# A softmax maximum by transposes, first rows tile by tile, and a new order in a transformer block's forward and backward pass

## The chip, the cores and the metric

The kernel runs on one core of a Trainium2 chip. The metric is the device time of one execution in microseconds (us). A core has five engines with a queue each: TensorE (PE in the profile, its weight loads PEld), VectorE (DVE), ScalarE (ACT), GpSimd (POOL) and SyncE (SP), which only issues transfers. Every engine takes its instructions strictly in the order of its queue and waits on semaphores for the others.

## The reference

One transformer block over 2048 positions of width 512, its output, and the gradients of the input and of all weights for a given output gradient. In bf16:

```
ln1  = layernorm(x);  q, k, v = ln1 @ wqkv            # 32 heads of 16
logit[s, w] = q[s] . k[s - 2w] / 4,  w = 0..7          # a dilated window, masked where s - 2w < 0
attn = softmax over w;  o[s] = sum over w of attn[s, w] * v[s - 2w]
h    = x + o @ wo
out  = h + gelu(layernorm(h) @ w1 + b1) @ w2 + b2      # width 1792 inside
outputs: out, and d(x), d(wqkv), d(wo), d(w1), d(b1), d(w2), d(b2) for grad_out
```

The softmax runs over only eight values for each head and position.

## The kernel before

The positions are cut into four chunks of 512, each of four row tiles of 128. Every chunk passes through: layernorm and turning (`p1_ln`), projections (`p1_qkv`), windowed attention (`p1_attn`), its output (`p1_o`), `wo` and the second layernorm (`p1_h`), the feed-forward part forward (`p2_h`, `p2_out`), its derivative (`p2_dg`) and backward (`p2_bwd`), the backward attention (`p3_go`, `p3_dots`, `p3_bands`, `p3_gl1`); at the end come the weight gradients (`wg_ffn`), whose matmuls also fill TensorE beside the backward attention.

**Order and homes.** The Python code only describes operations: each call of `op` names an engine, a function that issues the instructions, and the buffers read and written. A planner's result is written into the file as two tuples: `TURN` is the order in which all operations are issued (so each engine's queue is the part of it that belongs to that engine), `HOMES` the address of every SBUF buffer and the PSUM bank (0 to 7) of every PSUM buffer, in the order in which buffers are made. With these tuples present nothing is planned at run time.

**First rows.** For chunk 0, `layernorm` takes statistics of each tile on VectorE (L577, L578), adds epsilon (ve, L583), raises to the power -1/2 on GpSimd (L585) for two tiles at a time, forms minus mean times deviation (nm, L586) on VectorE, and normalizes each tile with a scale and a bias (L596). `to_fm_pairs` turns the tiles two by two on TensorE (L628, 8 transposes into one bank) and ScalarE copies 1024 columns of a pair out. `spin` runs idle matmuls on zeros (L1283): `WARM` = (11, 4) says 11 at the very start and 4 behind the turning. A transpose and a copy bring the bias b1 into columns (L1306, L1307).

**Attention.** `dots` multiplies q by eight shifted views of k on VectorE (L672) and TensorE sums within heads (L679) into two PSUM banks `L`: partitions are 4 shifts by 32 heads, the two banks hold the other factor two of the eight shifts. The maximum over the shifts: ScalarE copies one bank (asb), VectorE takes the maximum of both (m1, L856, 128 partitions); ScalarE copies the upper 64 partitions down (m1h, L860), VectorE takes the maximum (m2, L861); ScalarE copies 32 partitions down (m2h, L865), VectorE again (m3, L866). TensorE subtracts it from both banks with a matrix of -1 (L870, two matmuls of 512 columns), ScalarE takes the exponential (L872), TensorE sums (L878), VectorE inverts and so on.

**Bands.** The products with shifted rows, forward (`o`) and backward (`q`, `v`, `k`), go through `band`, 64 times in all: rows come by a gather on GpSimd's queue, VectorE multiplies 4096 values for each partition (L698, 2.3 us), TensorE sums eight matmuls of 512 columns into a bank (L707), ScalarE copies the bank out (L712). Two bands (m = 0, 1) make one half of a chunk, which TensorE then turns back (L722, `unperm`).

**Other lines that are spoken of:** L804 and L821 projections, L956 and L958 first feed-forward matmul and the copy of its bank by ScalarE, L961 GELU, L1012 second feed-forward matmul, L926 addition of b2 to h, L650 and L615 other transposes, L1201 weight gradients.

Of the kernel before, what the change touches and what calls it, by code (L numbers as in the profile page):

```python
# [427 lines left out]
def kernel(  # L428
# [142 lines left out]
    def layernorm(c, src, MV, ST, VE, NM, R, mv, st, ve, nm, rs, dst, eng, n=TPC):  # L571
# [8 lines left out]
        for j0 in range(0, TPC, n):  # L580
# [4 lines left out]
            op("POOL", 1.1, lambda s=s: G.tensor_tensor(out=rs[:, s], in0=ve[:, s], in1=mhalf[:, 0:n], op=ALU.pow), r=[(VE, (c, j0))], w=[(R, (c, j0))], tag="pow")  # L585
            op("DVE", 0.16, lambda s=s: V.scalar_tensor_tensor(out=nm[:, s], in0=mv[:, s, 0], scalar=-1.0, in1=rs[:, s], op0=ALU.mult, op1=ALU.mult),  # L586
               r=[(R, (c, j0))] + [(MV, t) for t in ts], w=[(NM, (c, j0))], tag="nm")
        for j in range(TPC):
            t = c * TPC + j
            rk = [(src, j), (R, (c, j // n * n)), (NM, (c, j // n * n))]  # L590
# [4 lines left out]
            else:  # L595
                op("DVE", 0.36, lambda t=t, j=j: V.tensor_scalar(out=dst()[:, j, :], in0=src()[:, j, :], scalar1=rs[:, t:t + 1],  # L596
                                                                scalar2=nm[:, t:t + 1], op0=ALU.mult, op1=ALU.add),
# [22 lines left out]
    def to_fm_pairs(src, dst, tag):  # L620

        for jp in range(2):
            pt = ps_("pt" + tag, 1, "pt", 2)

            def tr(jp=jp, pt=pt):
                for dc in range(DC):
                    for j in range(2):
                        T.transpose(pt.bf()[:, dc * 256 + j * P:dc * 256 + (j + 1) * P], src()[:, 2 * jp + j, dc * P:(dc + 1) * P], ident[:])  # L628
            op("PE", 8 * XP, tr, r=[(src, 2 * jp), (src, 2 * jp + 1)], w=[pt], tag="xp" + tag, al=[dst])
            evict(dst, lambda jp=jp: dst()[:, :, jp * 256:(jp + 1) * 256], pt, lambda pt=pt: pt.bf().rearrange("p (a n) -> p a n", a=DC), 1024,  # L630
                  key=jp, tag="fm" + tag)
# [60 lines left out]
    def band(cf, R, sc, m, sgn, dst, at, sca, tag):  # L692
        pr = sb("prb" + tag, [P, 2, 4, 512], tag="prod", lim=4)
        o0 = (2 if sgn < 0 else 0) + 4 * m
        st = -1024 if sgn < 0 else 1024

        def prod():
            V.tensor_tensor(out=pr().rearrange("p a j (d h) -> p a j d h", h=H),  # L698
                            in0=_sub(R()[:, o0, 0:1], [[st, 2], [512, 4], [32, DH], [1, H]]),
                            in1=_sub(cf()[:, 2 * sc + m, 0, 0, 0:1], [[128, 2], [32, 4], [0, DH], [1, H]]), op=ALU.mult)  # L700
        op("DVE", tt_us(4096), prod, r=[R, cf], w=[pr], tag="prod" + tag)
        ps = ps_("bs" + tag, 1, "bs", 2)

        def sums():
            for hf in range(2):
                for j in range(4):
                    T.matmul(ps()[32 * j:32 * j + 32, :], lhsT=S32[:], rhs=pr()[:, hf, j, :], start=(hf == 0), stop=(hf == 1),  # L707
                             skip_group_check=True)
        op("PE", 0.45, sums, r=[CST, pr], w=[ps], tag="bsum" + tag, al=[dst])

        def out():
            A.activation(out=dst()[:, at, :].rearrange("p (h d) -> p h d", d=DH), in_=ps().rearrange("p (d h) -> p h d", h=H),  # L712
                         func=ACT.Copy, scale=sca)
        op("ACT", act_us(512), out, r=[ps], w=[(dst, at)], tag="sink" + tag)
# [860 lines left out]
```

## Time and profile before

| what | value |
|---|---|
| three runs | 584.12 us median (582.18 to 587.52) |
| the profiled execution | 582.24 us, span 580.5 us |
| granted TensorE clock, mean | 0.997 |
| TensorE busy | 556.8 us, 96% of the span |
| VectorE busy | 490.2 us, 84% |
| ScalarE busy | 351.6 us, 61% |
| GpSimd busy | 90.4 us, 16% |
| DMA | 150.99 MB, mean 260 GB/s |

The span runs from the first to the last instruction. In a timeline row stand the start, the length, engine, line, operation, output and inputs, the shape (partitions x elements), how many instructions are merged, and in brackets the idle time of the engine before it with what ended it. In a row of groups stand busy time, mean length in ns, and idle time before. A matmul of 512 columns shows 0.38 us from start to modelled end, but the next one starts 0.216 us after it.

### The profile page before, as it was taken

To read this page: it belongs to the slowest core of one execution; us is meant where nothing else is said; L and a number is where in the kernel's file an instruction comes from. 1 tells how busy PE (TensorE), PEld (TensorE's weight loads), DVE (VectorE), ACT (ScalarE), POOL (GpSimd) and SP (SyncE) were. 2 spreads that over 40 slices of the span, in tenths; PEclk is the share of its full clock that TensorE was granted. 3 is DMA by queue.
4 is the path that set the end of the run, shared out by engine and by line. 5 is a ranking of instruction groups with operands and counts; after the bars stand their busy time and mean duration, and the time that the engine had idled before them with its cause. 6 is when DMAs were issued, how large, how long until landed. Compare 5 with 4: busy or idle time off the path is not lost.

```text
span 580.5 us, 9212 instructions
## 1 busy us (share of the span) xinstructions
PE 556.8 (96%) x3525; PEld 261.3 (45%) x3579; DVE 490.2 (84%) x645; ACT 351.6 (61%) x517; POOL 90.4 (16%) x89
## 2 busy tenths in 40 slices
PE   7999989799899999999999999999999899999997
PEld 3454544244344444444545444444444446444443
DVE  7999799999999999789865999998998899973900
ACT  5588899998997885988453424136542455364111
POOL 3020605031000000000000100432421241400000
PEclk8999999999999999999999999999999999999999
DMA  8579699999999998989999989989989996879322
GB/s 256 148 254 322 230 260 355 250 189 299 227 260 269 244 279 131 258 239 273 282 233 273 324 298 283 311 316 292 345 342 314 322 311 244 313 235 362 114 73 72
DMA packets 163147, 150.99 MB, mean 260 GB/s; under 512 B 112768, under 2 KB 149536, under 8 KB 158240
## 3 DMA queue, kind: packets, MB, share of 16 engines
q1 hardware_dynamic: 156768, 103.22, 64.1%
q0 software_dynamic: 6336, 47.19, 23.1%
q8 instruction: 28, 0.46, 0.3%
q14 instruction: 15, 0.12, 0.1%
HBM read 78.25 MB, written 42.77 MB: 208 GB/s over the span
## 4 chain that ended last, share of the span: by engine, by line
PE 75%; issue 4%; DVE 4%; ACT 3%; DMA 2%; SPq 0%; ACTq 0%; DVEq 0%
PE ps L1201 25%; PE ps L1060 8%; PE ps L1012 8%; PE ps L1173 7%; PE ps L1037 7%; PE ps L956 6%; PE ps L707 4%; PE ps L1082 2%; PE ps L722 2%; DMA gk_d<-gks 1%; PE ps L679 1%; DVE prbo L698 1%; PE ps L918 1%; ACT xb L958 1%; PE ps L650 1%
## 5 line engine op out<-in xcount | busy, mean ns | idle before, releaser
L956 PE MATMUL ps<-ln2T,w 128*128 128x512 bf16 x224 | 53.5, 379 | 2.5 <-ACT xb L958 2.3
L1037 PE MATMUL ps<-goT,w2T 128*128 128x512 bf16 x215 | 54.1, 379 | 0.4
L1012 PE MATMUL ps<-w,gl 128*128 128x512 bf16 x217 | 51.9, 379 | 0.9 <-ACT xb L958 0.6
L1201 PE MATMUL ps<-gw1in,ln2b 128*128 128x512 bf16 (+1 forms) x256 | 52.6, 353 | 0.0
L1060 PE MATMUL ps<-w1T,xb 128*128 128x512 bf16 x220 | 50.6, 379 | 0.2
L1201 PE MATMUL ps<-gor,gw2in 128*128 128x512 bf16 x217 | 50.2, 379 | 0.4 <-issue 0.2
L1039 DVE SCALAR_TENSOR_TENSOR xb<-xb,ps 128x512 bf16<-128x512 bf16 x56 | 37.9, 683 | 14.6 <-PE ps L1037 13.6
L1173 PE MATMUL ps<-wqkvT,gqkvT 128*128 128x512 bf16 x184 | 42.7, 379 | 0.6 <-issue 0.3
L958 ACT ACTIVATE xb<-ps,b1c 128x512 bf16<-128x512 f32 x56 | 36.7, 686 | 7.3 <-PE ps L956 7.2
L698 DVE TENSOR_TENSOR prbk<-Rk,cfk 128x4096 bf16<-128x4096 bf16 x16 | 36.0, 2288 | 6.0 <-DMA Rk<-q_d,rowi 2.7
L564 ACT CAST wgs<-ps 128x512 bf16<-128x512 f32 (+1 forms) x30 | 16.6, 559 | 38.8 <-PE ps L1201 38.7
L698 DVE TENSOR_TENSOR prbv<-Rv,cfv 128x4096 bf16<-128x4096 bf16 x16 | 36.3, 2287 | 3.3 <-PE ps L1201 1.8
L698 DVE TENSOR_TENSOR prbq<-Rq,cfq 128x4096 bf16<-128x4096 bf16 x16 | 36.3, 2278 | 2.3 <-PE ps L707 0.8
L672 DVE TENSOR_TENSOR prf<-qt,kt 128x4096 bf16<-128x4096 bf16 x16 | 35.9, 2278 | 1.4 <-PE ps L707 0.7
L672 DVE TENSOR_TENSOR prb<-got,vw 128x4096 bf16<-128x4096 bf16 x16 | 36.1, 2280 | 1.2 <-DMA vw<-v_d 0.6
L698 DVE TENSOR_TENSOR prbo<-Ro,cfo 128x4096 bf16<-128x4096 bf16 x16 | 36.2, 2286 | 0.3
L661 POOL DMA_INDIRECT Rq<-k_d,rowi x8 | 15.5, 1940 | 130.2 <-PE ps L1012 103.4
L737 ACT ACTIVATE gyr<-ps,rstd 128x512 bf16<-128x512 f32 x32 | 21.9, 685 | 21.5 <-PE ps L1173 18.5
L1201 PEld LDWEIGHTS <-ln2b 128*128 128x128 bf16 x256 | 24.0, 98 | 23.8 <-issue 3.4
L956 PEld LDWEIGHTS <-w 128*128 128x128 bf16 x224 | 21.1, 98 | 29.9 <-issue 5.6
L980 ACT ACTIVATE xb<-xb 128x2048 bf16<-128x2048 bf16 (+1 forms) x16 | 27.1, 1695 | 11.9 <-DVE xb L979 11.9
L1201 PEld LDWEIGHTS <-gw2in 128*128 128x128 bf16 x224 | 21.2, 98 | 27.4 <-issue 3.4
(178 smaller groups left out, 1069.8 us busy)
## 6 DMA issues: line engine op xcount, KB each, us to landing
g_d<-xrg SPq DMA_DIRECT2D x12, 512.0 KB
gh_d<-xrh SPq DMA_DIRECT2D x12, 512.0 KB
gw2in<-g_d SPq DMA_DIRECT2D x3, 2048.0 KB
gw1in<-gh_d SPq DMA_DIRECT2D x3, 2048.0 KB
ln_d<-ln SPq DMA_DIRECT2D x8, 512.0 KB
w<-in_B_w_dram SPq DMA_DIRECT2D x2, 1792.0 KB
out_dram<-wgs SPq DMA_DIRECT2D x13, 256.0 KB
v_d<-tmv SPq DMA_DIRECT2D x8, 256.0 KB
```

Source lines behind the costliest of these rows:

```text
L672: op("DVE", tt_us(4096), lambda g=g, pr=pr: V.tensor_tensor(out=pr(), in0=ql()[:, g, :].unsqueeze(1).to_broadcast([P, W, 512]), in1=_sub(k ...
L698: V.tensor_tensor(out=pr().rearrange("p a j (d h) -> p a j d h", h=H), in0=_sub(R()[:, o0, 0:1], [[st, 2], [512, 4], [32, DH], [1, H]]), i ...
L707: T.matmul(ps()[32 * j:32 * j + 32, :], lhsT=S32[:], rhs=pr()[:, hf, j, :], start=(hf == 0), stop=(hf == 1), skip_group_check=True)
L956: T.matmul(ps(), lhsT=w1()[:, dc, f * P:(f + 1) * P], rhs=cols(ln2T[c], dc, c in FM2), start=(dc == 0), stop=(dc == DC - 1))
L958: op("ACT", act_us(512, 1), lambda f=f, ps=ps, xb=xb, f0=f0: A.activation(out=xb()[:, f - f0, :], in_=ps(), func=ACT.Identity, bias=b1c[:, ...
L980: op("ACT", act_us(N), lambda xb=xb: A.activation(out=fl(xb), in_=fl(xb), func=ACT.Tanh, scale=GC), w=[xb], tag="tanh", mode=2)
L1012: T.matmul(ps(), lhsT=d["g"][f // 4]()[:, f % 4, j * P:(j + 1) * P], rhs=w2()[:, f, :], start=(f == 0), stop=(f == FT - 1))
L1037: T.matmul(ps(), lhsT=w2T()[:, dc, f * P:(f + 1) * P], rhs=goT()[:, dc, :], start=(dc == 0), stop=(dc == DC - 1))
L1039: op("DVE", 0.70, lambda f=f, ps=ps, z=z, f0=f0: V.scalar_tensor_tensor(out=z()[:, f - f0, :], in0=z()[:, f - f0, :], scalar=1.0, in1=ps() ...
L1060: T.matmul(ps(), lhsT=d["d"][f // 4]()[:, f % 4, j * P:(j + 1) * P], rhs=w1T()[:, f, :], start=(f == 0), stop=(f == FT - 1))
L1173: T.matmul(ps(), lhsT=d["gqkv"]()[:, b, j * P:(j + 1) * P], rhs=wqkvT()[:, b, :], start=(i == 0 and b == ks[0]), stop=(i == 2 and b == ks[ ...
L1201: T.matmul(ps()[:, 0:N], lhsT=l, rhs=r, start=(n == 0), stop=(n == k - 1))
```

## The change

- Softmax maximum: m1h, m2, m2h and the old m3 are gone. TensorE turns m1 in four transposes into a PSUM bank (xpm); one VectorE reduction with a negated maximum over the four shifts reads that bank and gives m3, now 128 positions by 4 tiles by 32 heads. The subtraction becomes 32 matmuls of 128 columns with the new m3 as weights, each into 32 output partitions.
- First rows: chunk 0 forms its deviations for three tiles and then for one; a tile is turned alone (`to_fm_tiles`) and copied alone, the fourth copy on VectorE. Where VectorE normalizes, it subtracts the mean and multiplies by the deviation as two scalars, and nm is no longer formed.
- Bands: `bands` makes both products and both sums of a half and then one ScalarE operation: a single instruction over both banks where these are neighbours, else two.
- The bias transpose (b1t, b1c) moves behind the first rows; `WARM` becomes (17, 4).
- `TURN` and `HOMES` are replaced as a whole (1988 operations instead of 2029).

```diff
-    def layernorm(c, src, MV, ST, VE, NM, R, mv, st, ve, nm, rs, dst, eng, n=TPC):
+    def layernorm(c, src, MV, ST, VE, NM, R, mv, st, ve, nm, rs, dst, eng, split=0):
...
-        for j0 in range(0, TPC, n):
+        first = [split if split and j >= split else 0 for j in range(TPC)]
+        for j0 in sorted(set(first)):
+            n = first.count(j0)
...
+            if "ACT" in eng:
+                op("DVE", 0.16, lambda s=s: V.scalar_tensor_tensor(out=nm[:, s], in0=mv[:, s, 0], scalar=-1.0, in1=rs[:, s], op0=ALU.mult, op1=ALU.mult),
...
-                op("DVE", 0.36, lambda t=t, j=j: V.tensor_scalar(out=dst()[:, j, :], in0=src()[:, j, :], scalar1=rs[:, t:t + 1],
-                                                                scalar2=nm[:, t:t + 1], op0=ALU.mult, op1=ALU.add),
+                op("DVE", 0.36, lambda t=t, j=j: V.tensor_scalar(out=dst()[:, j, :], in0=src()[:, j, :], scalar1=mv[:, t, 0:1],
+                                                                scalar2=rs[:, t:t + 1], op0=ALU.subtract, op1=ALU.mult),
...
+    def to_fm_tiles(src, dst, tag):
+        for j in range(TPC):
             pt = ps_("pt" + tag, 1, "pt", 2)
+            def tr(j=j, pt=pt):
                 for dc in range(DC):
+                    T.transpose(pt.bf()[:, dc * P:(dc + 1) * P], src()[:, j, dc * P:(dc + 1) * P], ident[:])
+            op("PE", DC * 0.057, tr, r=[(src, j)], w=[pt], tag="xp" + tag, al=[dst])
+            evict(dst, lambda j=j: dst()[:, :, j * P:(j + 1) * P], pt, lambda pt=pt: pt.bf()[:, 0:512].rearrange("p (a n) -> p a n", a=DC), 512,
+                  key=j, eng="DVE" if j == 3 else "ACT", tag="fm" + tag)
...
+    def bands(cf, R, sc, sgn, dst, at, sca, tag):
+        two = []
+        for m in range(2):
...
+        def out():
+            p0, p1 = two
+            if abs(p1.home - p0.home) == 1:
+                A.activation(out=dst()[:, at:at + 2, :].rearrange("p m (h d) -> p m h d", d=DH),
+                             in_=_sub(p0(), [[(p1.home - p0.home) * BANK, 2], [1, H], [H, DH]]), func=ACT.Copy, scale=sca)
+                return
+            for m in range(2):
+                A.activation(out=dst()[:, at + m, :].rearrange("p (h d) -> p h d", d=DH), in_=two[m]().rearrange("p (d h) -> p h d", h=H),
+                             func=ACT.Copy, scale=sca)
+        op("ACT", 2 * act_us(512), out, r=two, w=[(dst, at), (dst, at + 1)], tag="sink" + tag)
...
-        m1, m1h, m2, m2h, m3 = sb("m1", [P, 512]), sb("m1h", [64, 512]), sb("m2", [64, 512]), sb("m2h", [32, 512]), sb("m3", [32, 512])
+        m1, m3 = sb("m1", [P, 512]), sb("m3", [P, 4, 32])
...
+        def turn():
+            for j in range(4):
+                T.transpose(mt.bf()[:, j * P:(j + 1) * P], m1()[:, j * P:(j + 1) * P], ident[:])
+        op("PE", 0.23, turn, r=[CST, m1], w=[mt], tag="xpm")
+        op("DVE", tt_us(512, True), lambda: V.tensor_reduce(out=m3(), in_=_sub(mt.bf()[:, 0:1], [[P, 4], [1, 32], [32, 4]]), axis=mybir.AxisListType.X,
+                                                            op=ALU.max, negate=True), r=[mt], w=[m3], tag="m3")
         def sub():
             for hf in range(2):
-                T.matmul(L()[:, hf * 512:(hf + 1) * 512], lhsT=nSum4[0:32, :], rhs=m3(), start=False, stop=True, skip_group_check=True)
+                for j in range(4):
+                    for w4 in range(4):
+                        T.matmul(L()[32 * w4:32 * w4 + 32, hf * 512 + j * P:hf * 512 + (j + 1) * P], lhsT=m3()[:, j, :], rhs=ident[:],
+                                 start=False, stop=True, skip_group_check=True)
...
-WARM = (11, 4)
+WARM = (17, 4)
```

More of the change, by code (lines that the diff above doesn't have):

```diff
@@ L1304 @@
     load(B2C, lambda: b2bc[:], lambda: _ap(B_b2, [[0, P], [1, D]]), 128, tag="b2")
-    pb = ps_("pb1")
-    op("PE", 0.1, lambda: T.transpose(pb.bf()[:, 0:FT], b1b[:], ident[0:FT, 0:FT]), r=[B1B], w=[pb], tag="b1t")
-    op("DVE", 0.2, lambda: V.tensor_copy(out=b1c[:], in_=pb.bf()[:, 0:FT]), r=[pb], w=[B1C], tag="b1c")
     for c in range(NC):
```

77 lines of the change are left out of this document (29 added, 48 removed), and 249 rows, old and new, of tables (HOMES, TURN).

## The prediction

> **What bounds the kernel now.** I read the page first (span, busy shares, chain), then the busy time in stretches of 20 us, then the timeline of the stretches in which TensorE (PE) falls short, and last the groups of instructions by line and shape for the durations.
>
> ```profile
> span 580.5 us, 9212 instructions
> ...
> PE 556.8 (96%) x3525; PEld 261.3 (45%) x3579; DVE 490.2 (84%) x645; ACT 351.6 (61%) x517; POOL 90.4 (16%) x89
> ...
> PE 75%; issue 4%; DVE 4%; ACT 3%; DMA 2%; SPq 0%; ACTq 0%; DVEq 0%
> ```
>
> TensorE is busy for 556.8 of 580.5 us, and the chain that ended last runs over it for 75%. So 23.7 us are all that can be won without taking work from TensorE, and the question is where they lie.
>
> ```profile
> 0.00:20.00 20.00, 15.72 (x69) 7.31 (x71) 15.88 (x43) 10.79 (x22) 4.99 (x23) 0.91 0.73 212
> ...
> 100.00:120.00 20.00, 16.16 (x112) 6.81 (x112) 19.42 (x24) 19.13 (x23) 2.27 (x2) 1.00 1.11 259
> ...
> 140.00:160.00 20.00, 16.99 (x84) 7.32 (x85) 19.79 (x36) 19.88 (x22) 0.00 (x0) 1.00 0.95 234
> ...
> 460.00:480.00 20.00, 18.23 (x143) 8.90 (x143) 19.13 (x15) 8.83 (x16) 7.38 (x6) 1.00 0.89 317
> ...
> 560.00:580.00 20.00, 16.73 (x76) 7.45 (x76) 0.00 (x0) 4.50 (x8) 0.00 (x0) 1.00 0.19 66
> ```
>
> The columns after the length are busy time of PE, its weight loads, DVE (VectorE), ACT (ScalarE) and POOL (GpSimd), then granted clock and DMA. Five stretches hold 16.2 us of the 23.7: 4.3 at the start, 3.8 at 100 to 120, 3.0 at 140 to 160, 1.8 at 460 to 480, 3.3 at the end. At 100 to 120 DVE is full, at 140 to 160 DVE and ACT both are. The waits themselves:
>
> ```profile
> 106.84 0.61 PE L707 MATMUL ps<-prbo,S 128*32 128x512 bf16 x8 [1.59 <-DVE prbo L698]
> ...
> 109.04 0.62 PE L707 MATMUL ps<-prbo,S 128*32 128x512 bf16 x8 [0.61 <-DVE prbo L698]
> 111.24 0.61 PE L707 MATMUL ps<-prbo,S 128*32 128x512 bf16 x8 [1.59 <-DVE prbo L698]
> ...
> 156.70 1.02 PE L956 MATMUL ps<-ln2T,w 128*128 128x512 bf16 x4 [2.35 <-ACT xb L958]
> ...
> 159.80 1.46 PE L1012 MATMUL ps<-w,gl 128*128 128x512 bf16 x6 [0.56 <-ACT xb L958]
> ...
> 462.71 1.05 PE L707 MATMUL ps<-prbk,S 128*32 128x512 bf16 x16 [1.66 <-DVE prbk L698]
> ```
>
> Until 111 us TensorE waits for VectorE's band products of the third chunk (L698): up to there VectorE's queue sets the pace, and only what shortens that queue counts. At 156 us TensorE waits for ScalarE to empty a bank (L958): there ScalarE's queue counts. From 160 on a microsecond of TensorE work is a microsecond of span.
>
> **The start.**
>
> ```profile
> 1.87 3.97 PE L1283 MATMUL ps<-wz 128*128 128x512 bf16 x11 [1.87 <-DVE wz L1284]
> ...
> 6.41 0.17 DVE L583 TENSOR_SCALAR ve<-mv 128x2 f32<-128x2 f32 x1
> ...
> 7.38 0.18 PE L1306 MATMUL ps<-ident,b1b 14*128 14x14 bf16 x1 [1.54 <-POOL rstd L585]
> 7.59 0.17 DVE L1307 CAST b1c<-ps 128x14 f32<-128x14 bf16 x1 [0.98 <-PE ps L1306]
> ...
> 7.87 0.73 DVE L596 TENSOR_SCALAR ln<-xt,rstd,nm 128x512 bf16<-128x512 bf16 x2
> ...
> 8.34 2.20 PE L628 MATMUL ps<-ident,ln 128*128 128x128 bf16 x16 [0.78 <-DVE ln L596]
> ...
> 9.62 1.96 ACT L564 COPY ln1T<-ps 128x1024 bf16<-128x1024 bf16 x2 [3.35 <-PE ps L628]
> ...
> 10.33 1.66 PE L1283 MATMUL ps<-wz 128*128 128x512 bf16 x4
> ...
> 11.83 5.34 PE L804 MATMUL ps<-ln1T,wqk 128*128 128x512 bf16 x23
> ...
> 16.53 2.29 DVE L672 TENSOR_TENSOR prf<-qt,kt 128x4096 bf16<-128x4096 bf16 x1 [0.61 <-ACT qt L564]
> ```
>
> Before, VectorE's fourth statistic is done at 6.4, but its queue then stands behind the bias copy (L1307, behind a transpose that waits for a load) and the two small nm steps, and the first row tile is normalized only at 7.87. The change moves the bias copy behind the first dots and drops nm. Three of the four tiles now take their deviation from one POOL step that starts before the fourth statistic is done. I put the first normalization just behind that statistic, at 6.7, and the end of the fourth at 8.2 (four at the 0.36 of L596, with the POOL step for the fourth tile beside them). Each tile is then turned by itself: four transposes, and a 512-column copy of some 0.6 instead of 0.98 (half of 1.96). Two transpose banks are shared, so tile 2 waits for copy 0 (8.4) and tile 3 for copy 1 (8.9); the fourth copy is VectorE's and stands behind one statistic, so it ends at about 10.0. The six more idle matmuls cost 6 x 0.216 = 1.3 us of a TensorE that is idle there, ending at 7.1 instead of 5.84. The first projection starts at 10.1 to 10.6 instead of 11.83. The first dots follow 16.53 - 11.83 = 4.7 later, 14.8 to 15.3; but VectorE itself has its statistics and normalizations of the next chunk to do first, and reaches them at 15.3. **Gain 1.2 us** at the dots; bounds 0.5 and 1.7, and the reason for the lower one is the clock:
>
> ```profile
> 9.00:10.00 1.00, 1.00 (x11) 0.82 (x9) 1.00 (x3) 0.38 (x1) 0.00 (x0) 0.50 1.08 360
> ```
>
> The clock granted here is 0.50: TensorE had idled from 5.84 to 7.38 and again to 8.34, and all 16 transposes ran slow. If the longer warm-up does not hold the clock, the four idle matmuls after the last transpose take 1.66 again and the projection starts near 11.1. The Trainium skill (TensorE: Matmul & The Clock Gate, Part 1) says that the clock gate looks at free-running windows of about 3.4 us, so the moment of the drop varies from run to run; here it dropped after under 3 us of idling, which fits. By that rule both ends can occur, with no change to the sum. Loads: this row's 360 GB/s brings a 512 KB weight in about 1.5 us; the change puts one row load ahead of the weights and asks for the q weight first, in the order in which TensorE now uses them. I see them in time by under 1 us, and a late one is inside the bounds.
>
> **VectorE up to the last band product of chunk 3.** I read each engine's own order out of the two order lists. Up to that product the VectorE queue loses five nm, three m2, the 2048-wide addition of b2 (moved behind) and a small memset; it gains one copy of the first rows; m3 becomes a reduction out of PSUM.
>
> ```profile
> L586 DVE SCALAR_TENSOR_TENSOR nm<-mv,rstd 128x4 f32<-128x4 f32 x7 | 1.1, 152 | 1.1 <-POOL rstd L585 0.9
> ...
> L861 DVE TENSOR_TENSOR m<-m,m1h 64x512 bf16<-64x512 bf16 x4 | 1.6, 402 | 0.0
> ...
> L866 DVE TENSOR_TENSOR m<-m,m2h 32x512 bf16<-32x512 bf16 x4 | 1.6, 407 | 0.2 <-ACT m2h L865 0.2
> ...
> L856 DVE TENSOR_TENSOR m<-asb,ps 128x512 bf16<-128x512 bf16 x4 | 2.7, 680 | 0.0
> ...
> L926 DVE TENSOR_TENSOR h<-h,b2bc 128x2048 bf16<-128x2048 bf16 x4 | 4.9, 1213 | 0.0
> ```
>
> Removed: 5 x 0.15 + 3 x 0.40 + 1.21 = 3.2. Added: the reduction isn't in the trace; it reads 512 values of each partition from PSUM, and between the 0.41 of the step it replaces and 2 x 0.68 I take 0.68, the row that also reads 512 from PSUM: 3 x 0.27 = 0.8 (0 to 2.9). The copy is 0.6. So 3.2 - 0.8 - 0.6 = 1.8, of which the bias copy and the nm ahead of the dots (about 0.3) are already in the start. **Gain 1.5** (-0.6 to 2.3). The new chain m1, transposes, m3, sums crosses VectorE to TensorE and back; in the new order one to five matmul groups of 0.86 stand between, so TensorE has work, except in chunk 1 (one group), where it may wait 0.5 us under VectorE's cover. Without that cover it would be 4 x 0.5.
>
> The last product so comes 1.2 + 1.5 = 2.7 us earlier, and TensorE's 111.24 becomes 108.5.
>
> **ScalarE up to the second chunk's GELU (the wait at 156 to 160).**
>
> ```profile
> L865 ACT COPY m2h<-m 32x512 bf16<-32x512 bf16 x4 | 2.5, 617 | 0.1
> L860 ACT COPY m1h<-m 64x512 bf16<-64x512 bf16 x4 | 2.5, 617 | 0.1
> ...
> L712 ACT ACTIVATE ost<-ps 128x512 bf16<-128x512 f32 x16 | 9.2, 592 | 0.9 <-PE ps L707 0.8
> ```
>
> All eight m1h and m2h copies are gone, 8 x 0.617 = 4.9, and one 0.98 copy moves behind; 5.9 in all. The joint copy of two band sums saves little: the code makes it one instruction only where both banks are neighbours, and walking the list of homes in the order in which buffers are made, I find that in 6 of the 32 pairs; the other 26 still issue two of 0.59. With 6 x 0.2 it is 1 us of the whole, off the path. ScalarE had 3.0 idle in 100 to 160, so part of the 5.9 turns into idling, and TensorE arrives 2.7 earlier itself: ScalarE gains 5.9 - 2.7 = 3.2 on it, more than the 2.35 + 0.56 = 2.91 of the wait. But the new order puts two of chunk 4's band sums there instead of one, and VectorE, 19.79 of 20 busy, has little to spare for the second, so I count 2.0 of the 2.9 as won. **Gain 2.0** (0 to 2.9).
>
> **TensorE's own work.** Added are 4 transposes for each chunk, and 32 sums of 128 columns in place of two of 512.
>
> ```profile
> 32.58 0.60 PE L870 MATMUL ps<-m,nSum 32*128 32x512 bf16 x2
> 33.12 1.04 PE L821 MATMUL ps<-wv,ln1T 128*128 128x512 bf16 x4
> 33.99 1.06 PE L615 MATMUL ps<-ident,ln 128*128 128x128 bf16 x16
> 34.88 1.89 PE L821 MATMUL ps<-wv,ln1T 128*128 128x512 bf16 x8
> 36.70 0.29 PE L878 MATMUL ps<-e,S 128*32 128x128 bf16 x8
> 36.93 0.62 PE L650 MATMUL ps<-Pmat,kt 128*128 128x128 bf16 x8
> ```
>
> By the starts, two sums of 512 hold TensorE for 0.54, a full transpose 0.89 / 16 = 0.056, and eight sums of 128 columns into 32 output rows 0.23. The new sums have just this last shape, so 32 cost 0.9; the bounds are 0.54 (as little as the old ones) and 32 x 0.056 = 1.8 (one after another). One chunk costs 0.9 - 0.54 + 0.22 = 0.6 more. For chunks 1 to 3 VectorE's queue covers it; chunk 4's lies behind 111 us and counts. **Loss 0.6** (0.2 to 1.5; 2.4 if the cover is gone). Against it speaks a figure of the Trainium skill (TensorE: Matmul & The Clock Gate, Back-to-back issue gap): small matmuls that each load weights sustain about 81 ns at 128 columns. By that the 32 would take an estimated 2.6, and the loss for chunk 4 would be 2.3 instead of 0.6.
>
> **The rest of the order.** From 160 to 440 the trace shows TensorE waiting for nothing that matters, and the new order moves the same work by a few positions; the last 45 weight-gradient steps stand last in both, so the end is the same. Of the stores on POOL's queue two move behind the last gathers; what reads them is only these last steps. The 1.66 at 462 may go or come twice. **Zero**, bounds 1.7 either way.
>
> **Sum.** -1.2 - 1.5 - 2.0 + 0.6 = -4.1 us. The profiled execution took 582.24, 1.74 around its span of 580.5, so 578.1. The three runs shown have a median of 584.12 (582.18 to 587.52): the profiled one lies 1.9 below it, so against the median the same sum is about 1%.
>
> **The rivals.**
>
> *More is won.* The gains at their good ends, the added work as counted: 1.7 + 2.3 + 2.9 + 1.66 - 0.6 = 8.0, so 574.3. For it: 5.9 us leave a full ScalarE and one order was found for all of it. Against it: TensorE can't go under its own 556.8.
>
> *The waits come back.* In the new order two of chunk 4's band sums instead of one stand where TensorE so far waited for ScalarE. If VectorE is over 1 us late with both, it costs the 2.0 and 2.5 of new waits in the place of the one removed: -2.7 + 0.6 + 2.5 = 582.6. For it: VectorE is 19.79 of 20 busy there. Against it: its queue has become shorter too.
>
> *Slower: the joint copy.* Before, a band's bank was free 0.59 after its own sum; now both banks of a pair stay held until ScalarE has copied after the second sum, 1.2 for the two copies. Products come 2.29 apart, a sum takes about 0.55, so the next pair's first sum finds its bank free only if ScalarE starts within 2.29 - 0.55 - 1.2 = 0.5 us. From there each microsecond of lateness is one of TensorE, whose queue stands behind the sum. At 100 to 120 ScalarE is 19.13 of 20 busy, with steps of about 1 us; at 460 to 480 it is 8.83. If half of the 32 pairs lose 0.5, that is 8: 582.24 - 4.1 + 8 = 586.1.
>
> *The small sums don't run side by side.* At 0.056 one after another, and without VectorE's cover, each chunk costs 1.25 more than I count, and chunks 1 to 3 also their 0.6: -4.1 + 4 x 1.25 + 3 x 0.6 = +2.7, so 584.9. For it: nothing of this shape with a new weight each time is in the trace. Against it: the 0.23 for eight. The figure of the skill given above would make this rival worse: by it each chunk would cost 1.7 above my count, an estimated 587.
>
> **How the numbers follow.** Forecast 0.45 (2 to 6 us won), more won 0.22, waits come back 0.13, the joint copy 0.13, small sums one after another 0.07. A measurement of this kernel can tell about 1% from no change, 5.8 us of 584.12, so faster means under 578.3: half of the forecast and all of the first rival, 0.45. Within 1%: the other half, the waits, and half of the last rival, 0.39. Slower: the joint copy beyond half its price and what else I don't see, 0.16. The forecast's own range is 576 to 580. The range for 8 in 10 goes from 570.5, where beside the first rival's gains most small waits vanish too, to 587, just beyond the joint copy's 586.1.
>
> **What would show it.** Right: the first projection (L804) at 10.1 to 10.6 and the first dots at about 15.3; granted clock 1.00 from 7 us on; the last product of chunk 3 summed near 108.5; no wait above 1 us for ScalarE between 140 and 160; the 32 small sums within 0.9 us of TensorE; the reduction near 0.68. Wrong: waits of band sums for ScalarE's copy (the joint copy), waits of band sums for VectorE around 150, small sums 0.056 apart, or a start that is earlier while the dots are not.

## The result and the profile after

Over 20 executions of each, the changed kernel has a median of 582.34 us (576.43 to 588.14) and the kernel before 584.21 us (580.94 to 589.75); the ratio is 0.9942, with an interval of 0.9913 to 0.997. That is 0.6% faster: the outcome that the prediction calls within 1% and gave 0.39, behind the 0.45 for faster. The median lies above the forecast's own range of 576 to 580 us and inside the one for 8 in 10. The profiled execution took 576.73 us (span 575.0) against 582.24, a difference of 5.5 us where the sum had 4.1; the medians lie only 1.9 us apart.

Three lines of the page after: the span, the busy times, and the shares of the chain that ended last.

```profile
span 575.0 us, 9529 instructions
...
PE 561.8 (98%) x3721; PEld 264.3 (46%) x3721; DVE 488.7 (85%) x637; ACT 344.5 (60%) x504; POOL 84.3 (15%) x89
...
PE 82%; issue 6%; DMA 5%; ACT 3%; POOL 2%; SPq 1%; DVE 0%; POOLq 0%; ACTq 0%
```

TensorE's idle time has gone from 23.7 to 13.2 us. The 23.7 were somewhat too many: the page of before has 3525 matmuls for 3579 weight loads, so some records are missing there, and part of the 5 us by which the busy time has grown is no work. VectorE is hardly in the chain any more; DMA now is. The busy time in the same stretches of 20 us:

```profile
0.00:20.00 20.00, 17.42 (x79) 7.72 (x80) 16.59 (x40) 10.41 (x24) 5.04 (x23) 1.00 0.80 237
100.00:120.00 20.00, 17.74 (x117) 7.88 (x116) 19.79 (x24) 19.90 (x25) 3.96 (x5) 1.00 1.11 266
140.00:160.00 20.00, 18.76 (x106) 8.07 (x104) 19.53 (x35) 19.89 (x22) 0.00 (x0) 1.00 1.03 232
460.00:480.00 20.00, 19.25 (x133) 9.88 (x132) 18.25 (x13) 7.30 (x17) 8.31 (x5) 1.00 0.88 314
```

TensorE idles 2.6 instead of 4.3 us at the start, 2.3 instead of 3.8 at 100 to 120, 1.2 instead of 3.0 at 140 to 160 and 0.75 instead of 1.8 at 460 to 480. The rows of the timeline that answer to those of before (first projection, first dots, last band sum of chunk 3, the places of the waits for ScalarE, the wait at 462):

```profile
10.99 4.49 PE L821 MATMUL ps<-ln1T,wqk 128*128 128x512 bf16 x20 [0.71 <-DMA wqk<-in_A_wqkv_dram]
15.70 4.49 DVE L674 TENSOR_TENSOR prf<-qt,kt 128x4096 bf16<-128x4096 bf16 x2 [0.34 <-ACT kt L564]
108.93 0.61 PE L714 MATMUL ps<-prbo,S 128*32 128x512 bf16 x8 [0.62 <-ACT ost L725]
151.06 1.90 PE L973 MATMUL ps<-ln2T,w 128*128 128x512 bf16 x8 [0.95 <-DMA ln2T<-ln]
156.03 1.89 PE L1029 MATMUL ps<-w,gl 128*128 128x512 bf16 x8
465.94 0.61 PE L714 MATMUL ps<-prbq,S 128*32 128x512 bf16 x8 [0.75 <-DVE prbq L703]
```

The wait of 2.35 for ScalarE is gone, and a wait for a transfer (the transposed ln2 of the third chunk) stands near its place.

**Executions by their clock.** Each execution lists its mean granted clock. I put the executions of before that were run beside the experiments (104, on four chips) and the changed kernel's (32, in two sets) into classes by it; these means keep every execution, while the ratio above leaves out those more than 1.5% over the fastest.

| mean granted clock | before: executions, mean us | after: executions, mean us | difference |
|---|---|---|---|
| 0.999 to 1.000 | 15, 581.36 | 8, 576.98 | -4.38 |
| 0.996 to 0.998 | 30, 582.47 | 10, 580.48 | -1.99 |
| 0.993 to 0.995 | 15, 584.24 | 10, 583.46 | -0.78 |
| below 0.993 | 44, 585.20 | 4, 586.01 | +0.81 |

At a full clock the change wins 4.4 us, close to the 4.1 of the sum. In executions with a lower clock the gain melts away. So two questions were open: which part of the change made the 4.4, and what takes them back in many executions.

### The profile page after: what moved, and what is told of

Its sections match the earlier page's. It is cut to its first block, busy times and chain, and to the rows that moved or that the text cites. A ratio compares the mean times of both kernels' runs of the same rounds, so it can differ in the third digit from the quotient of the medians.

```text
span 575.0 us, 9529 instructions
## 1 busy us (share of the span) xinstructions
PE 561.8 (98%) x3721; PEld 264.3 (46%) x3721; DVE 488.7 (85%) x637; ACT 344.5 (60%) x504; POOL 84.3 (15%) x89
## 4 chain that ended last, share of the span: by engine, by line
PE 82%; issue 6%; DMA 5%; ACT 3%; POOL 2%; SPq 1%; DVE 0%; POOLq 0%; ACTq 0%
PE ps L1217 23%; PE ps L1029 8%; PE ps L1077 8%; PE ps L973 8%; PE ps L1054 7%; PE ps L1189 5%; PE ps L821 4%; PE ps L714 4%; PE ps L1099 2%; PE ps L681 2%; DMA ln2T<-ln 2%; PE ps L735 2%; PE ps L838 2%; PE ps L935 2%; PE ps L652 1%
## 5 line engine op out<-in xcount | busy, mean ns | idle before, releaser
L1077 PEld LDWEIGHTS <-xb 128*128 128x128 bf16 x224 | 21.9, 98 | 25.9
L1054 PEld LDWEIGHTS <-w2T 128*128 128x128 bf16 x224 | 21.7, 98 | 25.8 <-issue 0.8
L1029 PEld LDWEIGHTS <-gl 128*128 128x128 bf16 x224 | 21.7, 98 | 25.7 <-issue 0.4
```

What stands on the lines that cost most here:

```text
L1029: T.matmul(ps(), lhsT=d["g"][f // 4]()[:, f % 4, j * P:(j + 1) * P], rhs=w2()[:, f, :], start=(f == 0), stop=(f == FT - 1))
L1054: T.matmul(ps(), lhsT=w2T()[:, dc, f * P:(f + 1) * P], rhs=goT()[:, dc, :], start=(dc == 0), stop=(dc == DC - 1))
L1077: T.matmul(ps(), lhsT=d["d"][f // 4]()[:, f % 4, j * P:(j + 1) * P], rhs=w1T()[:, f, :], start=(f == 0), stop=(f == FT - 1))
```

## The experiments

One table first, since most verdicts rest on it: for each profile the start of the first projection, the time from there to the last band sum of chunk 3, and from there to the end of the span, all in us.

| kernel | first projection | to last chunk 3 sum | to the end |
|---|---|---|---|
| before | 11.83 | 99.4 | 469.3 |
| after | 10.99 | 97.9 | 466.1 |
| after, once more | 12.15 | 97.9 | 466.4 |
| new maximum, old order | 12.47 | 101.9 | 474.0 |
| both edits, old order | 10.93 | 101.7 | 469.0 |
| both edits, old order, mended | 11.91 | 103.2 | 468.9 |
| old maximum, new order | 10.41 | 103.3 | 469.8 |
| copies apart | 11.16 | 98.4 | 474.5 |
| dots early | 11.89 | 98.1 | 471.3 |
| normalization early | 11.82 | 98.0 | 465.3 |
| three moves with the dots | 9.73 | 98.8 | 469.2 |
| one copy moved in before | 11.79 | 99.4 | 468.6 |
| w1's transpose moved | 11.73 | 99.6 | 465.9 |
| three moves with w1's transpose | 9.64 | 98.4 | 465.6 |

**1. The new maximum alone, in the old order.** The kernel before with m1, four transposes, the reduction and the small sums at the places of the old chain:

```diff
-m1, m1h, m2, m2h, m3, two sums of 512        (ScalarE copies twice)
+m1, xpm, m3 (reduction), 32 sums of 128
```

> The kernel before, in its own order, with the new softmax maximum alone (m1, four transposes, one reduction, 32 small sums). Theory A (ScalarE is freed of eight copies, and that ends its lateness): the two waits of TensorE for xb at 156 to 160, 2.91 us together, fall under 1; the start is as before (dots at 16.5); VectorE saves 3 x 0.13 up to the last band sum of chunk 3, which comes at 110.8 (110.3 to 111.2) instead of 111.24; the 32 sums hold TensorE for 0.56; span 578.2 (577.0 to 579.5) against 580.5. Theory O (the new order and homes made the gain, the edits themselves none): the waits at 156 to 160 stay above 2, the band sum at 111.2, span 580.5 within 0.6.

Measured: 586.13 us, ratio 1.0047 (1.0022 to 1.0071). A row of the TensorE timeline and one of ScalarE's:

```profile
161.79 1.02 PE L957 MATMUL ps<-ln2T,w 128*128 128x512 bf16 x4 [2.35 <-ACT xb L959]
...
144.26 1.91 ACT L981 ACTIVATE xb<-xb 128x2048 bf16<-128x2048 bf16 x1 [1.60 <-DVE xb L980]
```

The wait for xb is 2.35 as before, to the hundredth, though all eight copies are gone. The second row says why. ScalarE itself stands idle there for 1.60 us, waiting for VectorE's product for the GELU's derivative; in the trace of before it is the same row at 139.17 with 1.59. From this point ScalarE is busy without a gap until the copy that TensorE waits for, and the last of the eight copies started at 122.93, ahead of this point. What was taken off ScalarE became waiting further up: at 122 to 130 it waits 4.0 us for TensorE where it waited 0.7 (1.7 us of slow clock, behind the last band sum, is part of that). Theory A falls here. The run is slower than either theory had it: the unperm transposes waited 1.57 us for the reduction, which I had put behind a band product, and the clock fell in four places (section on the hardware).

**2. Both edits, in the old order.** The same with the new first rows:

```diff
-layernorm in pairs, nm, to_fm_pairs, WARM = (11, 4)
+layernorm 3 + 1, no nm, to_fm_tiles, b1t behind the dots, WARM = (17, 4)
```

> The kernel before with the new maximum and the new first rows (split deviation, no nm, tile by tile turning, bias copy behind the dots, 17 idle matmuls), the k weight still asked for first, all else in the old order, b2's addition in its old place. Theory A: dots at 15.5 to 16.0; last band sum of chunk 3 at 111.24 - 0.83 (start) - 0.45 (nm) - 0.4 (maximum) = 109.6 (109.0 to 110.3), the rest of the 2.3 won there is the order's (b2's 1.21 moved behind); waits for xb at 156 to 160 under 1; span 577.0 (575.5 to 578.5). Theory O: only the start's 0.8 is won, span 579.7 (579 to 580.5), waits at 156 to 160 above 2.

Measured: 585.23, ratio 1.0017 (0.9992 to 1.0041).

```profile
10.93 6.22 PE L810 MATMUL ps<-ln1T,wqk 128*128 128x512 bf16 x28 [1.24 <-DMA wqk<-in_A_wqkv_dram]
...
55.35 0.61 PE L724 MATMUL ps<-ident,ost 128*128 128x128 bf16 x8 [1.57 <-DVE m L869]
...
112.62 0.61 PE L709 MATMUL ps<-prbo,S 128*32 128x512 bf16 x8 [1.59 <-DVE prbo L700]
158.32 1.02 PE L963 MATMUL ps<-ln2T,w 128*128 128x512 bf16 x4 [2.24 <-ACT xb L965]
```

The start came earlier by 0.9, but the last sum of chunk 3 came later than before (112.62 against 111.24), and the wait for ScalarE is 2.24. I put the loss down to my place for the reduction; the next run moves it.

**3. The same, mended.**

```diff
 VectorE's order, second chunk
-third band product, m3
+m3, third band product
```

> Both edits (new maximum, new first rows) in the old order once more, with one step mended: in the earlier run the second chunk's reduction stood behind a band product on VectorE, and the unperm transposes, which use the same bank, waited 1.57 us of TensorE for it; here the reduction goes in front of that product. Theory O (the edits by themselves are worth under 1 us, the rest of the gain is the new order's): the wait of 1.57 goes, the last band sum of chunk 3 comes at 111.0 (110.3 to 111.8), the wait for xb at 156 to 158 stays at 2.0 to 2.5, undisturbed span 580.2 (579.3 to 581.0), ratio to before 0.999 to 1.001. Theory A (the edits carry the gain): band sum at 109.6 or earlier, wait at 156 under 1.3, undisturbed span 577.5 (576.5 to 578.8), ratio 0.995 or less.

Measured: 585.17, ratio 1.0043 (1.0018 to 1.0069).

```profile
11.91 7.90 PE L810 MATMUL ps<-ln1T,wqk 128*128 128x512 bf16 x27 [2.43 <-DVE ve L585]
...
115.09 0.62 PE L709 MATMUL ps<-prbo,S 128*32 128x512 bf16 x8 [1.59 <-DVE prbo L700]
160.79 1.02 PE L963 MATMUL ps<-ln2T,w 128*128 128x512 bf16 x4 [2.28 <-ACT xb L965]
```

The wait of 1.57 is gone; VectorE stood 0.89 for the transposes instead. The first projection waited 2.43 for its weight (the row names VectorE, but the weight load of that line waits 2.9 us for the transfer of wqk) and the clock fell behind it, so the sum at 115.09 holds about 1.7 of slow clock; even without that, 101.5 us lie between the first projection and that sum, 2 more than before. Theory O holds in its waits. In the time it expected a ratio of 0.999 to 1.001, and the edits lose 0.4% here; in run 2 the interval still includes no change.

**4. The old maximum in the new order.**

```diff
-xpm, m3 (reduction), 32 sums of 128
+m1h, m2, m2h, m3, two sums of 512
```

> The changed kernel in its new order with the old chain for the maximum (m1, copy of 64 rows, m2, copy of 32 rows, m3, two sums of 512) put back at the places of the transposes and the reduction. Theory A: ScalarE has its eight copies of 0.617 again and TensorE waits for ScalarE or VectorE 1 to 3 us more, most of it between 85 and 160; last band sum of chunk 3 at 109.3 (109 to 111); span 577.5 (576.3 to 579.5) against 575.0. Theory O: the new order alone holds the gain, span 575.0 within 0.7.

Measured: 582.16 us, ratio 0.9986 (0.9963 to 1.0009). A row of the timeline and two stretches:

```profile
33.23 0.59 PE L887 MATMUL ps<-m,nSum 32*128 32x512 bf16 x2 [2.42 <-DVE m L883]
...
35.00:36.00 1.00, 1.00 (x4) 0.30 (x2) 1.00 (x3) 0.00 (x0) 0.94 (x2) 0.50 0.00 0
140.00:160.00 20.00, 19.63 (x104) 8.69 (x103) 19.67 (x39) 19.67 (x21) 1.63 (x2) 1.00 0.96 244
```

With the eight copies back on ScalarE, TensorE idles only 0.37 us at 140 to 160: no wait for ScalarE came back. TensorE gets there 4.8 us later than in the changed kernel (last sum of chunk 3 at 113.73 against 108.93), which could by itself hide eight copies of 0.617, so it is run 1 that decides against A. The span of 583.5 is beyond both theories: the time is lost elsewhere. In the new order the sums stand so close behind m1 that the old chain, which crosses between VectorE and ScalarE four times, leaves TensorE waiting 2.42 and 1.21 us, and the clock drops to 0.50 behind the first: 5.3 us in all, about what the last sum of chunk 3 comes later in the table. Behind that sum 3.7 more are lost, with waits of 2.8 for band products at 443 to 474, where the changed kernel has 0.75, and of 1.2 for a load. The new maximum is worth its latency, and only in an order that uses it.

**5. Separate copies of the band sums.**

```diff
-out() behind both sums: one instruction over two neighbouring banks, or two
+out() behind each sum, one bank each
```

> The changed kernel with a copy for each band of its own, issued behind that band's sum, instead of one operation behind both sums. Theory A (the joint copy is worth nothing either way): ScalarE's busy time grows by 6 x 0.2 = about 1.0, waits of TensorE for banks that ScalarE empties (0.62 at 108.9) go to under 0.2, span 575.0 within 0.6. Rival J (both banks held until the second sum cost time): span lower by 0.6 or more, the product queue reaches its last chunk 3 sum before 108.5. Rival S (six saved instructions on a full ScalarE count): span higher by 0.6 or more, new waits for ScalarE at 100 to 160.

Measured: 581.09, ratio 0.9946 (0.9915 to 0.9976), the changed kernel's own. From the timeline:

```profile
109.51 0.62 PE L712 MATMUL ps<-prbo,S 128*32 128x512 bf16 x8 [0.62 <-DVE prbo L702]
...
156.97 3.59 PE L965 MATMUL ps<-ln2T,w 128*128 128x512 bf16 x8 [5.77 <-DMA ln2T<-ln]
```

At 109 the same 0.62 us stand there with both banks free, now put down to the product: it was VectorE's wait all along. The joint copy is worth nothing that these runs can tell, either way. The 5.77 for the transposed ln2 had nothing to do with the edit and opened the second question. The DMA share and GB/s (last two columns) ahead of it:

```profile
138.00:140.00 2.00, 2.00 (x11) 0.93 (x10) 1.97 (x7) 2.00 (x2) 0.00 (x0) 1.00 1.62 69
140.00:142.00 2.00, 2.00 (x20) 1.26 (x18) 1.97 (x3) 1.75 (x4) 0.00 (x0) 1.00 0.87 19
142.00:144.00 2.00, 2.00 (x11) 0.88 (x9) 2.00 (x4) 1.98 (x3) 0.00 (x0) 1.00 1.39 58
144.00:146.00 2.00, 2.00 (x11) 0.92 (x10) 2.00 (x6) 2.00 (x2) 0.00 (x0) 1.00 1.30 36
```

For 8 us the transfer engines are full and move 19 to 69 GB/s, where the changed kernel's profile has 274 to 320 from 138 to 144.

**6. The changed kernel once more, and three moves in its order.** These four ran beside each other.

> The changed kernel itself, once more, beside the three that follow. The runs so far show that ScalarE's lateness at 156 is not a matter of its eight copies (it came back to the hundredth of a microsecond without them), and that the changed kernel's executions lie 3 us apart for each 0.003 of granted clock, where those of before lie about 1.2 apart. Theory D: the new order has put the transpose of ln2 of the third chunk (behind the last normalization, behind a GELU) so close to its use at 151 that any late transfer is a wait of TensorE and a drop of the clock. It expects a spread of 575 to 586 us of span, median near 580.5, and, in this profile, the wait at 151 for ln2T at 0.9 or more. Rival C (the clock falls on its own, anywhere): the same spread, with the drops elsewhere than behind that wait.

Measured: 580.44 us, ratio 0.9933 (0.9898 to 0.9968), executions from 576.35 to 585.86. The profile waited 0.74 for ln2T and showed no drop of the clock. The first projection waited 1.93 for its weight and started at 12.15, and from there on the run is the earlier one to within 0.3 us.

```diff
 VectorE's order (dots early)
-recip, stats of h, ve, dots 3, nm, ..., dots 4
+recip, dots 3, stats of h, ve, dots 4, nm, ...
```

> The changed kernel with two dots of the third chunk moved ahead on VectorE, the third in front of the statistics of h that wait 1.75 us for ScalarE at 65.4, the fourth in front of nm that waits 0.94 for GpSimd at 72.0. Theory V (VectorE's queue sets the pace up to the last band sum of chunk 3): that sum comes 2.2 us earlier, at 106.7 (106.2 to 107.5), and the span of an undisturbed execution is 573.0 (572.3 to 574.0) against 575.0. Rival P (TensorE's own order and ScalarE set it): the sum moves by less than 0.8 and new waits stand in other places; span 575.0 within 0.7.

Measured: 582.3, ratio 0.9938 (0.99 to 0.9975). Two TensorE rows of this run:

```profile
11.89 4.49 PE L821 MATMUL ps<-ln1T,wqk 128*128 128x512 bf16 x20 [1.77 <-DMA wqk<-in_A_wqkv_dram]
...
110.03 0.62 PE L714 MATMUL ps<-prbo,S 128*32 128x512 bf16 x8 [0.62 <-DVE prbo L703]
```

98.1 us lie between them, where the unmoved order has 97.9. VectorE's wait of 1.75 us is gone, the one for GpSimd is still there (0.93), and two new waits of TensorE of 0.94 and 0.30 for ScalarE stand at 77 to 81. Counted from the first projection, VectorE is 1.5 us ahead of the unmoved order at its dots of 86.66 (88.47 in the profile of the unmoved order). Then it waits 0.36 for ScalarE at 91.51, and before the last four products it waits once more:

```profile
100.95 9.02 DVE L703 TENSOR_TENSOR prbo<-Ro,cfo 128x4096 bf16<-128x4096 bf16 x4 [1.40 <-DMA Ro<-v_d,rowi]
```

It is the gather of the rows that comes last now. Theory V falls, because it left that gather out; P, that TensorE and ScalarE set the pace, has its new waits, but the one that ended last is a transfer's. The span of 581.3 says nothing on either: it has 2.6 us of waits for band products at 440 to 471 and the slow transfers of run 8's place. Why the gather's rows come no sooner is left open.

```diff
 ScalarE's order (normalization early)
-GELU (with its table load), last normalization of chunk 3
+last normalization of chunk 3, GELU
```

> The changed kernel with the last normalization of the third chunk's h moved in front of the GELU and its table load on ScalarE (3.1 us earlier), so that the transpose of ln2 starts about 3 us earlier. Theory D: the wait for ln2T at 151 (0.95) goes, an undisturbed execution has 574.1 (573.4 to 574.8), and executions with a lower clock become fewer: the median falls below that of the changed kernel beside it by 2 us or more. Rival C: the wait goes, the span falls by 0.9 at most, and the median by no more than 1.

Measured: 582.98, ratio 0.9943 (0.9906 to 0.998). In the profile the wait for ln2T is gone and the rest of the order is 0.8 us shorter (465.3), as expected. The median did not fall, and 7 of 12 executions lie below a clock of 0.996: the spread is not that wait alone. Theory D, as I put it, falls.

```diff
 SyncE's order (in addition to both moves above)
-zero rows, third row load, q weight
+q weight, zero rows, third row load
```

> The two moves above together, and the q weight asked for one row load earlier (the first projection waited 0.7 for it). If V and D hold: first projection at 10.3 to 10.6, last band sum of chunk 3 at 106.5 (106.0 to 107.5), no wait for ln2T above 0.3, span of an undisturbed execution 571.9 (571 to 573.3), median 3 us or more below the changed kernel's. If only D holds: 574 and a median 2 us lower. If neither: 575 within 0.7.

Measured: 579.62, ratio 0.9908 (0.9879 to 0.9938). A TensorE row of the start, and one further on with the transfer behind it (SPq is SyncE's queue):

```profile
9.73 4.80 PE L821 MATMUL ps<-ln1T,wqk 128*128 128x512 bf16 x20
...
133.79 2.27 SPq L559 DMA_TRANSPOSE w1T<-in_B_w_dram  x1
...
141.83 6.79 SPq L559 DMA_TRANSPOSE ln2T<-ln  x1
...
152.10 2.73 PE L973 MATMUL ps<-ln2T,w 128*128 128x512 bf16 x8 [2.42 <-DMA ln2T<-ln]
```

The span is 577.7, none of the outcomes that I had listed. The weight is there in time and the start is earlier by 1.3 us than in the changed kernel's first profile, 2.4 than in its second. But ln2T is 2.42 late although its normalization is early: its transpose took 6.79 us. The stretches ahead of it look like those of run 5:

```profile
138.00:140.00 2.00, 2.00 (x15) 1.06 (x14) 1.97 (x3) 1.75 (x4) 0.00 (x0) 1.00 1.42 35
140.00:142.00 2.00, 2.00 (x17) 1.12 (x15) 1.97 (x3) 1.98 (x4) 0.00 (x0) 1.00 0.98 30
```

What is special at this place? The new order issues a transpose of w1 (133.79) just beside chunk 4's gather (134.09 on GpSimd). In the kernel before that transpose is through at 136.94 and the gather is issued at 137.04. Three of the seven profiles with this pair side by side (run 5, and the first and third moves above) show two or more stretches of 2 us in a row with full transfer engines and under 70 GB/s, always here; none of the other seven shows two in a row, though single ones of 64 to 66 GB/s stand elsewhere, in the kernel before at 230.

**7. One copy moved in the kernel before.** To see what the old wait at 156 was:

```diff
 ScalarE's order, kernel before
-square (1.5 us), square (1.5 us), copy of the bank
+copy of the bank, square, square
```

> The kernel before with one move in ScalarE's order: the copy of the second chunk's first linear output that empties the bank for which TensorE waits at 156.7 goes in front of the two squares of 1.5 us that stood before it. Nothing else is changed, none of the eight m1h and m2h copies removed. Theory Q (the wait of 2.35 is a matter of what stands in front of that one copy, not of ScalarE's load): the wait falls under 0.4, at most 1 of it comes back by 161, span of an undisturbed execution 578.6 (577.8 to 579.5) against 580.5. Rival A (ScalarE is late as a whole): the wait goes to the next copies and the span stays at 580.5 within 0.6.

Measured: 584.04, ratio 1.0004 (0.9973 to 1.0035).

```profile
159.90 2.32 PE L1012 MATMUL ps<-w,gl 128*128 128x512 bf16 x10 [3.16 <-ACT xb L958]
```

The wait of 2.35 is gone and the next one has grown from 0.56 to 3.16. Rival A holds here: from 139 on ScalarE is late as a whole, and moving one copy helps nothing.

**8. The transpose of w1 away from the gather.**

```diff
 SyncE's order, changed kernel
-transpose of w1 at 134, ..., transpose of ln2, store, transpose of w1
+transpose of ln2, store, transpose of w1, transpose of w1
```

> The changed kernel with one transpose of w1 (the one issued at 134.5 beside chunk 4's gather) moved behind the next one, at 150, so that no transpose runs beside the gather, as it was before the change. Theory T (gather and transpose disturb each other): the gather's packets are through in 4.3 to 5.5 us (before: 4.5; runs of the changed order: 4.3 to 14), no 2 us in which 256-byte packets take over 200 ns, the transpose of ln2 takes 1.8, and slow executions become fewer: median 578.5 (577 to 580) against 580.4 to 582.3. Rival C: the gather is quiet, but the spread of 576 to 586 and the median stay within 1 us.

Measured over 6 executions: 578.53 us (577.27 to 579.06), ratio 0.9883 (0.986 to 0.9907).

```profile
11.73 6.18 PE L821 MATMUL ps<-ln1T,wqk 128*128 128x512 bf16 x20 [2.20 <-DMA wqk<-in_A_wqkv_dram]
...
140.00:142.00 2.00, 2.00 (x11) 0.92 (x10) 1.97 (x5) 1.75 (x3) 0.00 (x0) 1.00 0.74 247
...
147.90 1.83 SPq L559 DMA_TRANSPOSE ln2T<-ln  x1
```

The transfers run at 247 GB/s in that stretch and the transpose of ln2 takes 1.83. The gather needed 6.4 us by its packets, a little more than I expected. The median came out as expected, and no execution lies below a clock of 0.996, where 14 of the changed kernel's 32 do. Six executions are few, and the interval still overlaps that of the changed kernel's second set (0.9898 to 0.9968). These runs were on another chip than that set, so the two are compared over the kernel before, which ran on both and spread on this chip from 581.0 to 589.1.

**9. Three moves together.**

```diff
 changed kernel
+q weight ahead of the third row load
+last normalization of chunk 3 ahead of the GELU
+transpose of w1 away from the gather
```

> The changed kernel with three moves: the q weight asked for one row load earlier, the last normalization of the third chunk in front of the GELU, and the transpose of w1 away from the gather. The early dots of the run above, which won nothing, are left out. If T holds: no wait for ln2T, first projection at 10.3 to 10.6, undisturbed span 573.5 (572.5 to 574.5), median 577 (575.5 to 579), ratio to before 0.989. If only the start and the normalization count: undisturbed 573.5 to 574.5 and the median near 580, as in the run with all three earlier moves.

Measured over 6 executions: 577.14 us (575.35 to 578.78), ratio 0.9869 (0.9844 to 0.9894). The first projection starts at 9.64, sooner than I expected, no wait for ln2T is left, and the span of the profile is 573.6. This version beats both kernels: its interval lies below both sets of the changed kernel. How much each of the three moves adds was not measured.

## Why the prediction was right, and where for the wrong reason

**The start (-1.2).** Measured -0.84 in the first profile (dots at 15.70); in the second the first projection starts at 12.15, later than before the change. The turning went as forecast, the clock held at 1.00, and then TensorE stood still: the step that failed is "I see them in time by under 1 us". The q weight came 0.71 to 2.20 us late in six of the seven profiles that ask for it behind the third row load. With the load one place earlier the dots come at 14.62, past the good end of my bounds.

**VectorE up to the last band product (-1.5).** From the first projection to that sum the profile has 97.9 instead of 99.4: the size is right to 0.1. Two rows of groups give the reduction as I priced it and the waits of the band sums:

```profile
L880 DVE TENSOR_REDUCE m<-ps 128x128 bf16<-128x512 bf16 x4 | 2.7, 684 | 0.5 <-PE ps L878 0.5
...
L714 PE MATMUL ps<-prbo,S 128*32 128x512 bf16 x128 | 9.1, 382 | 2.7 <-DVE prbo L703 1.6 <-ACT ost L725 0.6 <-ACT h L564 0.5
```

What VectorE does from the first dots to the start of the last four products shows how far the reason holds (us, from each trace):

| kernel | busy | idle |
|---|---|---|
| before | 81.2 | 4.6 |
| both edits, old order, mended | 81.1 | 6.8 |
| after | 79.1 | 5.0 |
| dots early | 79.2 | 5.1 |
| old maximum, new order | 79.5 | 9.9 |

In the changed kernel the queue did become shorter, by 2.0 us of work, as forecast. In the old order the edits leave its work as it was, and its waits grow by 2.2 us, the longest, 1.33, for a band sum of TensorE (0.65 before): there they bring no gain (runs 1 to 3). The largest single piece of work that went, the 1.21 of b2's addition, was moved by the new order. And run 6 took a wait out of the queue without a gain. So "only what shortens that queue counts" was too narrow: the waits inside the queue count as much, and the gather comes due right behind it.

**ScalarE and the wait at 156 (-2.0).** Measured -1.8 at 140 to 160. My step was that ScalarE gains the time of its eight copies. It doesn't: it waits 1.6 us for VectorE at 139, after all eight copies, and is a full queue from there (runs 1 and 7). What I added as a doubt, that the new order changes what stands there, is what is left: in the old order the wait stays at 2.24 to 2.35 whatever the edits (runs 1 to 3). That the 2.0 came out so close is luck. Order and homes were replaced together, and no run tells which of the two did it.

**TensorE's own work (+0.6).** Smaller. Starts around the transposes and the small sums of one chunk:

```profile
116.43 0.39 PE L878 MATMUL ps<-ident,m 128*128 128x128 bf16 x4
116.65 4.91 PE L1029 MATMUL ps<-w,gl 128*128 128x512 bf16 x22
121.49 0.63 PE L887 MATMUL ps<-ident,m 128*32 128x128 bf16 x32
122.06 1.47 PE L1029 MATMUL ps<-w,gl 128*128 128x512 bf16 x6
```

Four transposes hold it for 0.22, the 32 sums for 0.57 instead of the 0.54 of the two old ones: 0.25 more, at the good end of the bounds. Four sums into different output partitions do run side by side: four take 0.071 us, where one full transpose takes 0.056. The Trainium skill's figure of about 81 ns (TensorE: Matmul & The Clock Gate, Back-to-back issue gap) does not hold for this shape: here it is 18 ns each.

**The rest of the order (0, bounds 1.7).** The wait at 462 lost 0.9, inside the bounds.

**The rivals.** *The joint copy* is refuted by run 5, which has the same time without it. *More is won* (574.3) was 2.4 us below the profiled time and 8 below the median. *The small sums* are refuted by the rows above. *The waits come back* didn't happen in the way I described. What I missed is a wait that no row of before could show: the order moved a transpose beside a gather.

## What to carry to other kernels

A wait for a full engine is not the sum of what it did before: look back along its queue to the last place where it stood idle itself, because only work behind that place can shorten the wait. A shorter chain is worth something only in an order that uses it, so test an edit in both orders before pricing it. And after a new order, compare what each transfer queue has in flight together, not only what each engine does; a median that lies away from an undisturbed profile points there.

## What the runs showed of the hardware

**The clock falls behind waits shorter than 3 us, and a fall takes about 1.7 us of full clock away.** Four stretches of 1 us from run 1, the clock in the third column from the end:

```profile
10.00:11.00 1.00, 1.00 (x9) 0.91 (x10) 0.97 (x3) 0.70 (x1) 0.00 (x0) 0.50 1.09 353
116.00:117.00 1.00, 1.00 (x4) 0.30 (x2) 0.97 (x3) 1.00 (x4) 0.00 (x0) 0.50 1.04 200
164.00:165.00 1.00, 1.00 (x3) 0.30 (x2) 1.00 (x4) 0.97 (x3) 0.00 (x0) 0.50 1.15 217
471.00:472.00 1.00, 1.00 (x8) 0.70 (x7) 1.00 (x2) 1.00 (x3) 0.89 (x1) 0.50 0.04 16
```

Each of these falls lasts about 3.4 us at 0.50 (the one behind the 5.77 of run 5 twice as long), which takes 1.7 us or 0.003 of the span's mean clock; four of them give the 0.988 that this execution lists. They follow waits of TensorE of 2.20 (run 8), 2.35 (run 1), 2.41 (run 1), 2.42 (runs 4 and the last of 6), 2.43 (run 3), a group of 1.59, 0.61 and 1.59 (run 1) and, at the start of the kernel before, waits of 1.54 and 0.78; yet 2.35 in the profile of before, 2.24 in run 2, 2.28 in run 3 and 3.16 in run 7 had no fall behind them. So the length of the wait alone does not decide it here. The Trainium skill (TensorE: Matmul & The Clock Gate, Part 1) has free-running windows of about 3.4 us, which agrees with the length of each fall and with the chance in it.

**A transpose and a gather in flight together can choke the transfers.** In run 5, counted from the DMA records of the trace, 256-byte packets, whose median is 18 ns elsewhere, took 0.5 to 1 us in the mean in six of the seven microseconds from 139 to 146, and the gather, through in 4.5 us in the kernel before, took 14. It doesn't happen in every execution, and why the packets slow down so far is open. The Trainium skill (DMA: Bandwidth & Descriptors, Queues, rings and completion order) says that each DMA engine takes turns between queues packet by packet; that lets small packets wait for the gather's 10 KB ones, about 0.39 us each here, but not both of them for as long as the records show.

**Left open.** The clock classes say that the changed kernel loses about 3 us from class to class and the kernel before about 1.3. Fewer executions of the changed kernel lie below 0.996 (14 of 32, against 59 of 104), so it is not more falls but dearer ones that take the gain back, and why they are dearer was not shown. That moving the transpose narrows the spread was seen; that every low-clock execution of the changed kernel comes from that place was not, since most of them have no profile.
